# The last product split in K: ten chunks the ordinary way, six in seven block products of eight

## The chip, the cores and the metric

One core of one Trainium2 chip runs the whole program. The metric is the device time of one execution in microseconds (us). Five engines run their own instruction streams in order and wait for each other by semaphores: PE (matrix products, into accumulators in PSUM), DVE and ACT (elementwise work), POOL, and SP, whose queue issues the transfers here.

## The reference, cut to what matters

```
def reference(**kwargs):
    attn_out = _attn_ref(q, k, v)          # (2, 12, 448, 64), causal
    x = attn_out as (896, 768)             # 896 tokens, 768 features
    a = x @ w_a ; b = x @ w_b              # 768 -> 1536
    x = (a * b) @ w_out                    # 1536 -> 768
    h = x @ w_in                           # 768 -> 2048
    g = h * (1.0 / (1.0 + np.exp(-h)))
    return (g @ w_out2).astype(np.float32) # 2048 -> 768, the last product
```

The weights come as 64-bit floats and the result is 32-bit.

## The kernel before, in words

Features lie on the 128 partitions and tokens along the free dimension. The 896 tokens are two halves of 448 (`b` = 0, 1), a chunk is 128 features, so the last product has `NG` = 16 chunks of K and `NP` = 6 chunks of output. After the attention come four stages of products: 1 (`w_ab`), 2 (`w_mid`), 3 (`w_in`) and 4 (`w_out`, the last product). Every factor is held as two parts, a high and a low one, and each product of a chunk is three matmuls of 128x128 weights against 128x448 (high by high, high by low, low by high; L296).

Work on PE is cut into **granules**: two output chunks (`m`, `m+1`) and some chunks of K. There are two kinds.

- **Plain** (`plain`): for each chunk of K, two weight tiles by two token halves by three matmuls, 12 in all, into four accumulators that stay open over all granules of the same `m`. Stage 4 is all of this kind: for each of three `m`, four granules of four chunks. At the end of an `m`, `ending` copies each accumulator (L939, ACT) and sends it out (L940, SP queue). While `m` is 0, `hand_over` makes the high part (L771, ACT) and the low part (L774, DVE) of every chunk of activations, two chunks ahead of their use.
- **Fast** (`quad`): six chunks of K are three pairs, the two output chunks and the two token halves make the other two dimensions of a 2x2 block product, and seven products of blocks do the work of eight: 7 x 3 chunks x 3 matmuls = 63 instead of 72. Stage 3 and most of stage 1 are of this kind. It needs sums of activation blocks, split in high and low parts (`ACTS`, seven sets for each of three pairs), and sums of weight blocks (L279, L284, DVE). Its four results come out of copies of an accumulator (L319, ACT) and additions (L794, DVE). Activation sums for stage 1 are made by `sums_of`, driven by `Sums`.

The weights of each granule are loaded as raw 64-bit words (`load_ahead`, L141, SP queue) and converted two granules ahead of use: two ACT steps (L214, L220) and two DVE steps (L226, L231) for each of the two tiles, then high parts (L253, ACT) and low parts (L257, DVE). `Timeline` sets the order: its clock is the count of matmuls written so far, and each elementwise step is put into its engine's stream when its due count is reached (`CONV_F`, `CONV_X`, `CONV_Y` give the due points of the conversion as fractions of a granule) and when buffers are free (`A`, `W`, `R` and `banks` count them). The engines then run these streams in order.

Of the kernel before, what the change touches and what calls it, by code (L numbers as in the profile page):

```python
# [10 lines left out]
F32 = mybir.dt.float32  # L11
# [27 lines left out]
SUMS_MM = 3  # L39
# [9 lines left out]
POST = 9  # L49
HAND = 2  # L50
SLOT_MM = 7

CONV_F = dict(exp=(-0.06, 0.07), low=(0.01, 0.13), join=(0.20, 0.29), sign=(0.37, 0.45), t13=0.54, t24=0.62,
              wa=(0.58, 0.72), wd=(0.62, 0.80), wc=(0.74, 0.90), wb=(0.85, 1.0),
# [2 lines left out]
              wa=(0.44, 0.54), wd=(0.48, 0.59), wc=(0.56, 0.65), wb=(0.61, 0.71))  # L57
CONV_Y = dict(exp=(-0.54, -0.17), low=(-0.50, -0.10), join=(-0.22, 0.30), sign=(-0.14, 0.36), t13=0.62, t24=0.72,
              wa=(0.60, 0.80), wd=(0.66, 0.86), wc=(0.86, 0.98), wb=(0.93, 1.04))

@with_exitstack
def fused_kernel(ctx: ExitStack, tc: tile.TileContext, qk, v, w_ab, w_mid, w_in, w_out, out):
# [19 lines left out]
    NKB = (S + P - 1) // P  # L84
    NF, NG = w_ab.shape[0], w_in.shape[0]
    KP = NP // 2
    H = NP * P
    toks = [slice(b * S, (b + 1) * S) for b in range(B)]

# [10 lines left out]
    class Ring:  # L100


        def __init__(self, pools, sizes, shape, tag="t"):
            self.pools, self.room, self.shape, self.tag, self.home = pools, list(sizes), shape, tag, {}
# [295 lines left out]
    def sums_of(c):  # L400
# [40 lines left out]
        rest()  # L441
        A.free(s4)

    class Sums:


        def __init__(self):
            self.gens, self.need = [], 1

        def step(self):  # L450
            if not self.gens or self.need > A.left() - SPARE:
                return
            self.need = next(self.gens[0], None)
            if self.need is None:
                self.gens.pop(0)
                self.need = 1
                self.step()

        def go_on(self):
            self.step()  # L460
            if self.gens:
                line.after(SUMS_MM, self.go_on)

    sums_x = Sums()

    granules = []

    def granule(src, n, fast, **more):
        granules.append({"src": src, "n": n, "fast": fast, "length": 7 * 3 * KP if fast else 12 * n, **more})
# [7 lines left out]
    for m in range(0, NG, 2):  # L477
        granule([w_in[m], w_in[m + 1]], NP, True, stage=3, m=m)
    for m in range(0, NP, 2):
        for k in range(0, NG, 4):  # L480
            granule([w_out[m + i, :, k:k + 4] for i in range(2)], 4, False, stage=4, m=m, k=k, K=NG)

    for g in granules:
        if g["stage"] == 3 and g["m"] in (0, 2):
            g["due"] = (CONV_X, CONV_Y)[g["m"] // 2]
    loads += [(g, src) for g in granules for src in g["src"]]

    with tc.manual_schedule():  # L490
# [328 lines left out]
        def gate_put(g):  # L819
            def put(i, j, t):  # L820
                key = (g["m"] + j, i)
                psum = id(t) in banks.home
                if g["s"] == 0:
                    t_f[key] = t
                    if psum:
                        t_f[key] = copy_of(t, "ga")
                        banks.free(t)
                    return
                src = t[:, 0:S] if psum else t
                nc.vector.tensor_tensor(out=t_f[key], in0=src, in1=t_f[key], op=ALU.mult)  # L830
                (banks if psum else A).free(t)
            return put

        def silu_put(g):
            def put(i, j, t):
                key = (g["m"] + j, i)
                psum = id(t) in banks.home

                def act():
                    if psum:  # L840
                        g_f[key] = A.new(F32, "gf")
                        nc.scalar.activation(out=g_f[key], in_=t[:, 0:S], func=AF.Silu)
                        banks.free(t)
                    else:
                        nc.scalar.activation(out=t, in_=t, func=AF.Silu)
                        g_f[key] = t
                line.after(6 if i == 0 and j == 0 or psum else 3, act)
            return put

        def plain(g, accs, f, s, order, done):  # L850


            for bs, tiles in order:
                for k in range(g["n"]):
                    kk = g["k"] + k
                    if f and g["m"] == 0 and kk + HAND < g["K"]:
                        for b in range(B):
                            hand_over(f, s, (kk + HAND, b), 6 + 3 * b)
                    for i in tiles:
                        wh, wl = (t[:, k] for t in g["w"][i])  # L860
                        for n in range(3):
                            for b in bs:
                                ah, al = s[kk, b]
                                l, r = ((wh, ah), (wh, al), (wl, ah))[n]
                                mm(accs[i][b], l, r, kk == 0 and n == 0, kk == g["K"] - 1 and n == 2)
                        line.tick(3 * len(bs))
                    if g["m"] == NP - 2 and tiles[-1] == 1:
                        for b in bs:
                            A.free(*s.pop((kk, b)))
                for b in bs:  # L870
                    for i in tiles:
                        done(b, i)
            for t in g["tiles"].values():
                W.free(*t)
# [7 lines left out]
        for at, g in enumerate(granules):  # L882
            used += g["length"]
            if at + 2 < len(granules):
                line.convert(granules[at + 2], used - LEAD, granules[at + 1]["length"])
            load_ahead()
            stage, m = g["stage"], g["m"]
            if g["fast"]:
                f, s = (t_f, t_s) if stage == 1 else (g_f, g_s)
                last = at + 1 < len(granules) and not granules[at + 1]["fast"]  # L890
                if last:
                    for k in range(HAND):
                        for b in range(B):
                            line.after(42 + 6 * k + 3 * b, partial(hand_over, f, s, (k, b), 6))
                quad(g, gate_put(g) if stage == 1 else silu_put(g), last)
                continue
            if stage == 1:

                put, bs = gate_put(g), [0, 1]
                accs = [[None, None], [None, None]]  # L900
                if at == 0:
                    bs = [1]
                    for i in range(2):
                        line.after(6 * i, partial(put, 0, i, first[i]))
                for i in range(2):
                    for b in bs:
                        accs[i][b] = banks.new(F32, "acc")
                plain(g, accs, None, XS, [(bs, (0, 1))] if at == 0 else [((0, 1), (0,)), ((0, 1), (1,))],
                      lambda b, i: line.after(3 * b, partial(put, b, i, accs[i][b])))
                if at == 1:  # L910
                    line.to(line.now)
                    for k in range(0, NP, 2):
                        A.free(*XS[k, 1])
                continue
            f, s = (t_f, t_s) if stage == 2 else (g_f, g_s)
            last, end = m == NP - 2, g["k"] + g["n"] == g["K"]
            if g["k"] == 0:
                accs = [[banks.new(F32, "acc") for _ in range(B)] for _ in range(2)]
            def ending(b, i, acc, m=m, last=last):
                src = acc[:, 0:S]  # L920
                if stage == 2:
                    todo = []
                    combine(m // 2, f"A{b + 1}{i + 1}", src, keep, todo)
                    n = 0

                    def pay():
                        nonlocal n
                        if todo:
                            todo.pop(0)()
                            n += 1  # L930
                        if todo:

                            line.after(3 if not last else 12 if n > 1 and len(todo) == 1 else 0, pay)
                        else:
                            banks.free(acc)
                    pay()
                    return
                o = A.new(F32, "o")
                nc.scalar.copy(out=o, in_=src)  # L939
                nc.sync.dma_start(out=out[m + i, :, toks[b]], in_=o)  # L940
                A.free(o)
                banks.free(acc)

            def done(b, i):
                if end:
                    line.after(0 if last else (2 * b + i) * 6, partial(ending, b, i, accs[i][b]))
                    if last:
                        line.to(line.now)

            plain(g, accs, f, s, [((0,), (0, 1)), ((1,), (0,)), ((1,), (1,))] if last and end else [((0, 1), (0, 1))],  # L950
                  done)
# [43 lines left out]
```

## Time and profile before

| | |
|---|---|
| median of 3 runs | 561.45 us (561.14 to 562.01) |
| profiled execution | 561.41 us, its span 559.6 us |
| PE busy | 552.7 us, 99% of the span |
| DVE, ACT busy | 427.8 us (76%), 375.3 us (67%) |
| granted TensorE clock, mean | 0.999 |

The profiled execution's own time lies 1.81 us over the span, which runs from its first to its last recorded instruction or transfer. Durations of single matmuls overlap the next one, so the distance from start to start tells what one costs. The same holds for DVE and ACT: a step's duration is longer than the distance to the next step's start.

### The profile page before, as it was taken

The numbers are of one execution on the slowest core, as the hardware profiler recorded it, in microseconds if no ns is written. First come the engines' busy times: TensorE is split into PE (matmuls) and PEld (weight loads), VectorE is DVE, ScalarE is ACT, GpSimd is POOL, SyncE is SP. The second block draws the span as 40 slices with busy tenths as digits, with TensorE's granted clock in tenths as the row PEclk, the third lists the DMA queues.
The fourth block names the chain that finished last, engine by engine and source line by source line (L and its number), as shares of the span: only waits on it lengthen the run. The fifth ranks groups of instructions, "written<-read, shape, count | busy, mean of one in ns | idle before, by whom it ended". The sixth has DMA issues, their size and how long they took to land.

```text
span 559.6 us, 8368 instructions
## 1 busy us (share of the span) xinstructions
PE 552.7 (99%) x2978; PEld 493.6 (88%) x2978; DVE 427.8 (76%) x811; ACT 375.3 (67%) x736; POOL 72.2 (13%) x127
## 2 busy tenths in 40 slices
PE   8999999999999999999999999999999999999997
PEld 6777767999999999999999999999999999999996
DVE  5899998998989889879682888888885896442600
ACT  5989897756666666678654566877776995632601
POOL 5888874000000000000000000000000000000000
PEclk9999999999999999999999999999999999999999
DMA  7336323044333333333333342333332242631501
GB/s 248 121 113 216 116 83 126 1 132 164 123 145 115 114 112 114 112 114 112 114 112 114 112 147 80 113 114 119 143 126 83 76 152 76 216 117 45 168 0 66
DMA packets 18089, 65.41 MB, mean 117 GB/s; under 512 B 2176, under 2 KB 6784, under 8 KB 18048
## 3 DMA queue, kind: packets, MB, share of 16 engines
q1 hardware_dynamic: 18048, 64.89, 34.3%
q8 instruction: 23, 0.38, 0.3%
q14 instruction: 18, 0.15, 0.1%
HBM read 62.13 MB, written 2.75 MB: 116 GB/s over the span
## 4 chain that ended last, share of the span: by engine, by line
PE 94%; DVE 3%; issue 1%; POOL 1%; ACT 1%; DMA 1%; SPq 0%; DVEq 0%; ACTq 0%; POOLq 0%
PE acc L296 83%; PE pt L653 4%; PE xo L665 3%; PE sc L581 3%; PE sc L585 2%; DVE sm L604 1%; POOL p L621 1%; DMA k<-qk 1%; DVE ql L556 0%; DVE kl L556 0%; ACT p L608 0%; ACT ptr L746 0%; DVE wgbl L257 0%; SPq L539 0%; DVE sums L617 0%
## 5 line engine op out<-in xcount | busy, mean ns | idle before, releaser
L226 DVE SCALAR_TENSOR_TENSOR wq<-wr 128x768 uint32<-128x768 uint32 (+1 forms) x76 | 66.4, 875 | 26.2 <-ACT wr L220 25.4
L319 ACT COPY s<-acc 128x448 f32<-128x448 f32 x72 | 38.4, 533 | 60.2 <-PE acc L296 59.8
L220 ACT ACTIVATE wr<-wr,wbias 128x768 uint32<-128x768 uint32 (+1 forms) x76 | 69.8, 918 | 0.0
L214 ACT ACTIVATE wr<-wr 128x768 f32<-128x768 f32 (+1 forms) x76 | 63.8, 840 | 3.3 <-DMA wr<-w_out 1.8
L231 DVE SCALAR_TENSOR_TENSOR wq<-wr,wq 128x768 uint32<-128x768 uint32 (+1 forms) x76 | 63.8, 872 | 0.1
L621 POOL TENSOR_SCALAR p<-p,rcp 128x448 f32<-128x448 f32 (+6 forms) x84 | 56.2, 685 | 16.8 <-DVE rcp L618 7.3
L608 ACT ACTIVATE p<-sm,nmax 128x448 f32<-128x448 f32 (+6 forms) x84 | 42.0, 508 | 11.4 <-DVE nmax L604 10.8
L296 PE MATMUL acc<-th,wgbl 128*128 128x448 f32 x168 | 49.6, 366 | 0.0
L296 PE MATMUL acc<-tl,wgbh 128*128 128x448 f32 x168 | 49.4, 366 | 0.0
L296 PE MATMUL acc<-th,wgbh 128*128 128x448 f32 x168 | 49.4, 366 | 0.0
L296 PE MATMUL acc<-th,wgal 128*128 128x448 f32 x168 | 49.4, 365 | 0.0
L296 PE MATMUL acc<-tl,wgah 128*128 128x448 f32 x168 | 49.4, 365 | 0.0
L296 PE MATMUL acc<-th,wgah 128*128 128x448 f32 x168 | 49.3, 365 | 0.0
L604 DVE CUSTOM_DVE_ANT_0 sm<-sc,mask 128x448 f32<-128x448 f32 (+6 forms) x84 | 31.4, 417 | 6.0 <-PE sc L585 5.0
L296 PEld LDWEIGHTS acc<-th,wgbh 128*128 128x128 f32 x168 | 31.5, 188 | 2.9 <-DVE s L794 0.2
L296 PEld LDWEIGHTS acc<-th,wgah 128*128 128x128 f32 x168 | 31.6, 188 | 2.8
L296 PEld LDWEIGHTS acc<-th,wgbl 128*128 128x128 f32 x168 | 31.6, 188 | 2.6
L296 PEld LDWEIGHTS acc<-tl,wgah 128*128 128x128 f32 x168 | 31.5, 188 | 2.6
L296 PEld LDWEIGHTS acc<-th,wgal 128*128 128x128 f32 x168 | 31.6, 188 | 2.5
L296 PEld LDWEIGHTS acc<-tl,wgbh 128*128 128x128 f32 x168 | 31.5, 188 | 2.5
L257 DVE TENSOR_TENSOR wgal<-wq,wgah 128x512 fp32r<-128x512 f32 (+1 forms) x20 | 16.0, 802 | 23.1 <-ACT wgah L253 14.4
L653 PE MATMUL pt<-ident,p 128*128 128x128 f32 x192 | 27.8, 282 | 2.2 <-POOL p L621 1.3
(166 smaller groups left out, 1380.6 us busy)
## 6 DMA issues: line engine op xcount, KB each, us to landing
wr<-w_ab SPq DMA_DIRECT2D x24, 768.0 KB, 4.7
wr<-w_in SPq DMA_DIRECT2D x16, 768.0 KB, 4.9
wr<-w_out SPq DMA_DIRECT2D x24, 512.0 KB, 4.3
wr<-w_mid SPq DMA_DIRECT2D x12, 768.0 KB, 4.5
v<-v SPq DMA_DIRECT2D x12, 256.0 KB, 3.0
q<-qk SPq DMA_DIRECT2D x24, 112.0 KB, 2.9
k<-qk SPq DMA_DIRECT2D x12, 224.0 KB, 2.9
out<-o SPq DMA_DIRECT2D x12, 224.0 KB, 3.6
```

The source lines that it names most:

```text
L214: nc.scalar.activation(out=word(i, 1).bitcast(F32), in_=word(i, 1).bitcast(F32), func=AF.Copy, scale=2.0 ** -112)
L220: nc.scalar.activation(out=word(i, 0), in_=word(i, 0), func=AF.Relu, bias=wbias, scale=2.0 ** -29)
L226: nc.vector.scalar_tensor_tensor(out=xi(i), in0=word(i, 1), scalar=3, in1=word(i, 0), op0=ALU.logical_shift_left, op1=ALU.bitwise_or)
L231: nc.vector.scalar_tensor_tensor(out=xi(i), in0=word(i, 1), scalar=0x80000000, in1=xi(i), op0=ALU.bitwise_and, op1=ALU.bitwise_or)
L296: nc.tensor.matmul(out=acc[:, 0:S], lhsT=w, rhs=a, start=first, stop=last, skip_group_check=True)
L319: nc.scalar.copy(out=t, in_=acc[:, 0:S])
L581: nc.tensor.matmul(out=sc, lhsT=t[a][:, j - BIG].rearrange("p h q -> p (h q)"), rhs=t[k][:, 0:K], start=(i == 0), stop=(i == 2))
L604: nc.vector.tensor_tensor_reduce(out=sm, in0=sc, in1=mask[:, S - K:S], op0=ALU.add, op1=ALU.min, scale=-(D ** -0.5), scalar=3.0e38, accum_ ...
L608: nc.scalar.activation(out=p_sb[u % 2][j][:, 0:K], in_=sm, func=AF.Exp, bias=t["nmax"][:, c:c + 1], scale=-1.0, accum_out=t["sums"][:, c:c ...
L621: nc.gpsimd.tensor_scalar(out=pj, in0=pj, scalar1=t["rcp"][:, COL[j]:COL[j] + 1], scalar2=1.0, op0=ALU.mult, op1=ALU.mult,)
L653: nc.tensor.transpose(out=place[j, kb], in_=p_sb[u % 2][j][:, kb * P:(kb + 1) * P], identity=ident)
L665: nc.tensor.matmul(out=t["x"][h * D:(h + 1) * D, kb * P:S], lhsT=t["v"][:, kb, h * D:(h + 1) * D], rhs=t["pt"][:, kb, h, kb * P:S], start= ...
```

## The change

The last product is cut in K. Its first ten chunks (`N4` = `NG` - `NP` = 10) stay plain, in granules of four and six chunks for each of the three `m`; their sums are no longer sent out but copied to tiles `o` that stay on chip (`parts`). After all plain granules come three fast granules, one for each `m`, over the last six chunks. `out_put` adds each fast result to its `o` (L914, DVE) and sends it out. A new generator, `sums_last`, makes the activation sums of the six chunks while the plain granules run, driven by a second `Sums`; these six chunks need no `hand_over`. `CONV_Z` sets the due points of one conversion.

```
+PUT_MM = 20
+START_G = 60
+PACE_G = 3
+SPARE_G = 3
...
+CONV_Z = dict(exp=(0.02, 0.15), low=(0.09, 0.22), join=(0.35, 0.45), sign=(0.50, 0.58), ghi=(0.64, 0.72), glo=(0.78, 0.86))
...
+    N4 = NG - NP
...
+    def sums_last(c, f):
+
+        a11, a12, a21, a22 = (f.pop((N4 + 2 * c + i, b)) for b in range(B) for i in range(2))
...
+        yield 1
+        s3 = add(a11, a21, ALU.subtract)
+        yield 2
+        rest = halves_of(s3, 7)
+        yield 1
+        s1 = add(a21, a22, ALU.add)
+        A.free(a21)
+        yield 0
+        rest()
+        A.free(s3)
+        yield 2
+        rest = halves_of(a22, 4)
+        yield 1
+        s2 = add(s1, a11, ALU.subtract)
...
+        rest = halves_of(s1, 5)
+        yield 1
+        s4 = add(a12, s2, ALU.subtract)
...
+        for t, n in ((a11, 1), (a12, 2), (s2, 6), (s4, 3)):
+            yield 2
+            rest = halves_of(t, n)
+            yield 0
+            rest()
+            A.free(t)
...
-            if not self.gens or self.need > A.left() - SPARE:
+            if not self.gens or self.need > A.left() - self.spare:
...
-                line.after(SUMS_MM, self.go_on)
-
-    sums_x = Sums()
+                line.after(self.pace, self.go_on)
+
+    sums_x, sums_g = Sums(), Sums(SPARE_G, PACE_G)
...
     for m in range(0, NP, 2):
-        for k in range(0, NG, 4):
-            granule([w_out[m + i, :, k:k + 4] for i in range(2)], 4, False, stage=4, m=m, k=k, K=NG)
+        for k, n in ((0, N4 - 6), (N4 - 6, 6)):
+            granule([w_out[m + i, :, k:k + n] for i in range(2)], n, False, stage=4, m=m, k=k, K=N4)
+    for m in range(0, NP, 2):
+        granule([w_out[m + i, :, N4:] for i in range(2)], NP, True, stage=4, m=m)
...
+        if g["stage"] == 4 and g["m"] == 0 and not g["fast"] and g["k"]:
+            g["due"] = CONV_Z
...
+        parts = {}
+
+        def out_put(g):
+            def put(i, j, t):
+                key = (g["m"] + j, i)
+                psum = id(t) in banks.home
+
+                def add():
+                    o = parts[key]
+                    nc.vector.tensor_tensor(out=o, in0=t[:, 0:S] if psum else t, in1=o, op=ALU.add)
+                    (banks if psum else A).free(t)
+                    nc.sync.dma_start(out=out[key[0], :, toks[i]], in_=o)
+                    A.free(o)
+
+                line.after(0 if psum or g["m"] == NP - 2 else PUT_MM, add)
+                line.to(line.now)
+            return put
...
-                quad(g, gate_put(g) if stage == 1 else silu_put(g), last)
+                quad(g, (gate_put, None, silu_put, out_put)[stage - 1](g), last)
...
+            if stage == 4 and g["k"] == m == 0:
+                def begin():
+                    sums_g.gens += [sums_last(c, g_f) for c in range(KP)]
+                    sums_g.go_on()
+                line.after(START_G, begin)
...
-                o = A.new(F32, "o")
-                nc.scalar.copy(out=o, in_=src)
-                nc.sync.dma_start(out=out[m + i, :, toks[b]], in_=o)
-                A.free(o)
+                parts[m + i, b] = copy_of(acc, "o")
                 banks.free(acc)
```

Line numbers are shifted in the changed kernel: the matmul is L302, the conversion's ACT steps are L220 and L226, its DVE steps L232 and L237, `hand_over` is L826 and L829, the copy of an accumulator L325, the addition in `quad` L849; new are the additions and splits of `sums_last` (L456 on DVE, L461 on ACT, L462 on DVE) and L914. The instructions up to the first granules of stage 4 are in the same order in both kernels.

**First place: ACT at the start of stage 4.** `th` are the high parts of the first chunks, `wr` raw weights under conversion, `s` results of stage 3. Before:

```order
L319 COPY s_4668<-acc 128x448
L220 ACTIVATE wr<-wr,wbias 128x512
L771 CAST th<-s_3826 128x448
L214 ACTIVATE wr<-wr 128x512
L771 CAST th<-s_3860 128x448
L220 ACTIVATE wr<-wr,wbias 128x512
L845 ACTIVATE s_4668<-s_4668 128x448
L771 CAST th<-s_3909 128x448
L771 CAST th<-gf 128x448
```

With the change:

```order
L325 COPY s_4667<-acc 128x448
L220 ACTIVATE wr<-wr 128x768
L826 CAST th<-s_3826 128x448
L826 CAST th<-s_3860 128x448
L226 ACTIVATE wr<-wr,wbias 128x768
L220 ACTIVATE wr<-wr 128x768
L900 ACTIVATE s_4667<-s_4667 128x448
L226 ACTIVATE wr<-wr,wbias 128x768
L826 CAST th<-s_3909 128x448
L826 CAST th<-gf 128x448
```

The two last rows are the high parts of chunk 2: four conversion steps of 768 now stand between the copy and them, where three of 512 stood.

The same place on DVE with the change: `tl` are the low parts, `wq` the weights as 32-bit floats, and the rows end with both low parts of chunk 2.

```order
L829 TENSOR_TENSOR tl<-s_3860,th 128x448
L849 TENSOR_TENSOR s_4635<-acc,s_4635 128x448
L232 SCALAR_TENSOR_TENSOR wq<-wr 128x768 x2
L829 TENSOR_TENSOR tl<-s_3909,th 128x448
L237 SCALAR_TENSOR_TENSOR wq<-wr,wq 128x768
L829 TENSOR_TENSOR tl<-gf,th 128x448
```

One of the two conversion steps L237, which stood together ahead of the low parts, now stands between them.

**Second place: ACT where the fast granules of stage 4 begin.** Before there are none, and at the end of an `m` (here the first) the copies of results stand among conversion steps:

```order
L939 COPY o<-acc 128x448 x2
L253 CAST wgah<-wq 128x512
L939 COPY o<-acc 128x448
L253 CAST wgbh<-wq 128x512
L939 COPY o<-acc 128x448
```

With the change, at the end of the last plain `m`; `p1h` to `p7h` are high parts of the activation sums, `s_5419` is the first copy of the first fast granule:

```order
L461 CAST p1h<-s_4605 128x448
L325 COPY o<-acc 128x448 x2
L461 CAST p2h<-s_4635 128x448
L325 COPY s_5419<-acc 128x448
L325 COPY o<-acc 128x448
L461 CAST p6h<-S 128x448
L325 COPY o<-acc 128x448
L461 CAST p3h<-S 128x448
```

The last four parts of the third pair of chunks stand behind copies that wait for PE; on DVE `p6l<-S,p6h` needs `p6h`.

**Third place: the end.** Before, ACT ends with four copies, each followed by a transfer:

```order
L214 ACTIVATE wr<-wr 128x512
L220 ACTIVATE wr<-wr,wbias 128x512
L253 CAST wgah<-wq 128x512
L253 CAST wgbh<-wq 128x512
L939 COPY o<-acc 128x448 x4
```

With the change the results end on DVE:

```order
L849 TENSOR_TENSOR s_5699<-s_5688,s_5699 128x448
L914 TENSOR_TENSOR o<-s_5699,o 128x448
L849 TENSOR_TENSOR s_5676<-acc,s_5676 128x448
L914 TENSOR_TENSOR o<-s_5676,o 128x448
L914 TENSOR_TENSOR o<-acc,o 128x448
```

The last copy on ACT has become an addition on DVE out of the accumulator, behind four others.

## Rows read from the trace of the kernel before

**Rows 1.** Page, head and part 1: busy us, share of the span, instructions.

```profile
span 559.6 us, 8368 instructions
PE 552.7 (99%) x2978; PEld 493.6 (88%) x2978; DVE 427.8 (76%) x811; ACT 375.3 (67%) x736; POOL 72.2 (13%) x127
```

**Rows 2.** Chain that ended last, in order of time: start, us, what; its end.

```profile
98.67 457.62 PE acc L296 x2250
556.29 0.02 issue
556.31 0.53 ACT o L939
```

**Rows 3.** Timeline of PE (start, us, engine, line): first and last of stage 4.

```profile
438.97 0.57 PE L296 MATMUL acc<-th,wgah 128*128 128x448 f32 x2
...
555.91 0.37 PE L296 MATMUL acc<-th,wgbl 128*128 128x448 f32 x1
```

**Rows 4.** Timeline of ACT: the same copy in two neighbouring fast granules of stage 3.

```profile
402.63 0.53 ACT L319 COPY s<-acc 128x448 f32<-128x448 f32 x1 [0.21 <-PE acc L296]
...
415.42 0.54 ACT L319 COPY s<-acc 128x448 f32<-128x448 f32 x1 [0.22 <-PE acc L296]
```

**Rows 5.** Windows of stage 4: stretch, length, busy of each engine, PEclk, DMA share, GB/s.

```profile
440.00:500.00 60.00, 60.00 (x297) 55.31 (x296) 42.02 (x72) 40.92 (x75) 0.00 (x0) 1.00 0.41 138
500.00:540.00 40.00, 40.00 (x198) 36.95 (x197) 14.23 (x22) 14.22 (x24) 0.00 (x0) 1.00 0.28 89
540.00:559.60 19.60, 16.27 (x81) 14.68 (x79) 0.00 (x0) 2.13 (x4) 0.00 (x0) 0.98 0.13 47
```

**Rows 6.** Timeline of DVE: steps of 768, 384, 448 and 512 back to back.

```profile
406.38 0.95 DVE L257 TENSOR_TENSOR wal<-wq,wah 128x768 fp32r<-128x768 f32 x1
407.24 0.55 DVE L257 TENSOR_TENSOR wdl<-wq,wdh 128x384 fp32r<-128x384 f32 x1
407.71 0.95 DVE L257 TENSOR_TENSOR wcl<-wt,wch 128x768 fp32r<-128x768 f32 x1
...
441.34 0.62 DVE L774 TENSOR_TENSOR tl<-s,th 128x448 fp32r<-128x448 f32 x1
441.87 0.62 DVE L774 TENSOR_TENSOR tl<-gf,th 128x448 fp32r<-128x448 f32 x1
...
448.32 1.29 DVE L231 SCALAR_TENSOR_TENSOR wq<-wr,wq 128x512 uint32<-128x512 uint32 x2
449.52 0.61 DVE L774 TENSOR_TENSOR tl<-s,th 128x448 fp32r<-128x448 f32 x1
```

**Rows 7.** Timeline of ACT: conversion steps of 768, high parts, and a copy.

```profile
410.37 0.92 ACT L214 ACTIVATE wr<-wr 128x768 f32<-128x768 f32 x1
411.18 0.98 ACT L220 ACTIVATE wr<-wr,wbias 128x768 uint32<-128x768 uint32 x1
412.05 0.91 ACT L214 ACTIVATE wr<-wr 128x768 f32<-128x768 f32 x1
...
434.12 0.57 ACT L771 CAST th<-s 128x448 fp32r<-128x448 f32 x1
434.59 0.68 ACT L214 ACTIVATE wr<-wr 128x512 f32<-128x512 f32 x1
...
435.62 0.53 ACT L319 COPY s<-acc 128x448 f32<-128x448 f32 x1
436.04 0.78 ACT L220 ACTIVATE wr<-wr,wbias 128x512 uint32<-128x512 uint32 x1
```

**Rows 8.** Group of instructions by line and shape, 400 to 560: xcount | busy, mean ns.

```profile
L794 DVE TENSOR_TENSOR s<-acc,s 128x448 f32<-128x448 f32 x7 | 4.3, 618 | 2.5 <-PE acc L296 2.5
```

**Rows 9.** Timeline of ACT and the transfer queue at the end; DMA issues there.

```profile
550.82 1.14 ACT L939 COPY o<-acc 128x448 f32<-128x448 f32 x2 [15.02 <-PE acc L296]
...
551.38 5.82 SPq L940 DMA_DIRECT2D out<-o  x4
...
out<-o SPq DMA_DIRECT2D x4, 224.0 KB, 1.9
```

More of the change, by code (lines that the diff above doesn't have):

```diff
@@ L442, in sums_of, with add, halves_of, __init__ @@
         A.free(s4)
+    def sums_last(c, f):
+        a11, a12, a21, a22 = (f.pop((N4 + 2 * c + i, b)) for b in range(B) for i in range(2))
+        def add(a, b, op):
+            t = A.new(F32, "S")
+            nc.vector.tensor_tensor(out=t, in0=a, in1=b, op=op)
+            return t
+        def halves_of(t, n):
+            hi, lo = ACTS[n][c] = A.new(F32R, f"p{n}h"), A.new(F32R, f"p{n}l")
+            nc.scalar.copy(out=hi, in_=t)
+            return lambda: nc.vector.tensor_tensor(out=lo, in0=t, in1=hi[:].bitcast(F32), op=ALU.subtract)
+        yield 1
[14 more added lines that the diff above has]
+        rest()
+        A.free(a22)
+        yield 2
+        rest = halves_of(s1, 5)
+        yield 1
+        s4 = add(a12, s2, ALU.subtract)
+        yield 0
+        rest()
+        A.free(s1)
+        for t, n in ((a11, 1), (a12, 2), (s2, 6), (s4, 3)):
+            yield 2
+            rest = halves_of(t, n)
+            yield 0
+            rest()
+            A.free(t)
     class Sums:
-        def __init__(self):
-            self.gens, self.need = [], 1
+        def __init__(self, spare=SPARE, pace=SUMS_MM):
+            self.gens, self.need, self.spare, self.pace = [], 1, spare, pace
         def step(self):
-            if not self.gens or self.need > A.left() - SPARE:
+            if not self.gens or self.need > A.left() - self.spare:
                 return
@@ L889, in fused_kernel @@
                 f, s = (t_f, t_s) if stage == 1 else (g_f, g_s)
-                last = at + 1 < len(granules) and not granules[at + 1]["fast"]
-                if last:
+                last = at + 1 == len(granules) or not granules[at + 1]["fast"]
+                if last and stage < 4:
                     for k in range(HAND):
@@ L915, in fused_kernel @@
             f, s = (t_f, t_s) if stage == 2 else (g_f, g_s)
-            last, end = m == NP - 2, g["k"] + g["n"] == g["K"]
+            last, end = m == NP - 2 and stage == 2, g["k"] + g["n"] == g["K"]
+            if stage == 4 and g["k"] == m == 0:
[3 more added lines that the diff above has]
+                line.after(START_G, begin)
             if g["k"] == 0:
```

## The prediction

> **What bounds the kernel now.** Read first the busy shares on the page [rows 1], then the chain that ended last, in order of time [rows 2], then the windows of the stage that is changed [rows 5]. The shares say that PE is busy in 99% of the span. That alone could hide slow stretches, since pipelined matmuls overlap; the chain settles it. From 98.67 us to 556.29 us it is nothing but matmuls of L296, one after the other, and only a copy and a transfer follow [rows 2]. So in the last product the end is set by the count of matmuls times their distance from start to start. Stage 4 has 16 chunks x 12 matmuls x 3 values of `m` = 576 of them; the first starts at 438.97, the last at 555.91 [rows 3]. That is 575 distances in 116.94 us, 203.4 ns each, with no loss to be seen. The windows add that the other engines have room there: over 440 to 559.6 us DVE works 42.0 + 14.2 = 56.3 us and ACT 40.9 + 14.2 + 2.1 = 57.3 us [rows 5], and most of that lies ahead of 500 us. The granted clock is 1.00 in both full stretches, the higher level of 2.4 GHz [rows 5].
>
> The sum is made against the profiled execution, 561.41 us, which is 0.04 us under the median of 561.45 us; I carry no correction for that.
>
> **The change, PE.** Plain granules now hold ten chunks: 10 x 12 x 3 = 360 matmuls. Three fast granules add 3 x 63 = 189. Together 549, so 27 fewer. Is a matmul of a fast granule as cheap as a plain one? Two neighbouring fast granules of stage 3 have the same copy at 402.63 and 415.42 [rows 4]: 12.79 us for 63, 203.0 ns each. So 216 plain matmuls x 203.4 ns = 43.93 us go, 189 x 203.0 ns = 38.37 us come: **5.56 us** less on the path.
>
> The Trainium skill, page "TensorE: Matmul & The Clock Gate", section "Back-to-back issue gap", gives a warm spacing of N/2.4 + 2.5 ns, an estimate of 189 ns for 448 columns; 27 of these are 5.1 us, and the forecast would be 556.4 us by it. The measured 203 ns differs from it, and the measurement decides.
>
> **The change, the end.** Before, the last copy on ACT starts 0.40 us after the last matmul's start [rows 2, 3] and takes 0.53 us [rows 2]. Now a DVE addition out of the accumulator stands there, 0.618 us for the nearest row, an addition from an accumulator in `quad` [rows 8]: **+0.09 us**. Four DVE steps stand ahead of it (third place of the order). The two that add product 3 become possible 9 matmuls = 1.83 us before PE is done and take about 0.62 + 0.05 + 0.62 = 1.3 us; the other two belong to a product that ended 18 matmuls = 3.7 us before. So DVE waits for PE, not the reverse. The last transfer of 224 KB lands 1.9 us after its issue [rows 9], as before. The transfer ahead of it now comes some 1.2 us earlier instead of 2.4; but of the four transfers before two stood just as close, behind two copies that took 1.14 us together, and the median to landing is still 1.9 us [rows 9]. Cost nothing.
>
> **The change, DVE and ACT in total.** Distances from start to start on DVE: 0.86 us for a step of 768, 0.47 for 384, 0.53 for 448, (449.52 - 448.32)/2 = 0.60 for 512 [rows 6]. Before, stage 4 wants 32 low parts (17.0 us) and 12 conversions of six steps of 512 (43.2): 60.2 us, less the first conversion, which is done ahead of it (3.6): 56.6, against 56.3 measured. That agrees, so the same sum may be made of after: 20 low parts 10.6; three conversions with 512, 10.8; three with 768, 18 x 0.86 = 15.5; three for fast granules, each 7 x 0.86 + 5 x 0.47 = 8.4, so 25.1; activation sums, three times 4 additions and 7 low parts, 33 x 0.53 = 17.5; results, 3 x 7 additions x 0.53 = 11.1. Together 90.6, less 3.6: 87 us in a stage of 111.4 us, 78%. ACT has 12 fewer high parts but 21 for the sums and 12 more copies, and larger conversions; it ends near 70 us. No engine but PE is full over the stage, so what can cost time is the order at single places. I work out the two tightest.
>
> **Tight place one, start of stage 4** (first place of the order). PE reaches chunk 2 after 24 matmuls, at 438.97 + 4.88 = 443.85, and its fourth matmul needs the second low part at 443.85 + 0.61 = 444.46. ACT: the copy at 435.62 is set by PE and the next step starts at 436.04 [rows 7]. Then, with 0.81 us for L214 and 0.87 for L220 at 768 [rows 7] and 0.47 for a high part [rows 7], which I also take for the activation among them: 0.81 + 2 x 0.47 + 0.87 + 0.81 + 0.47 + 0.87 = 4.77, so 440.81; two high parts, the second done at about 441.85. DVE: its second L226 step (L232 after) waits for that last L220, about 440.95, then 0.86 (441.81), a low part (442.34), L231 (443.20), the second low part done by 443.82. PE wants it at 444.46: **0.6 us to spare**. Before it was done at 442.49, from the row at 441.87 [rows 6], 2 us to spare. So this cover shrinks, but holds; chunk 4, behind the rest of this conversion, is about as close. Price if I am off: a tenth more on these nine microseconds would make PE wait 0.3 us, twice 0.6.
>
> **Tight place two, first fast granule** (second place of the order). Call the end of the last plain granule P, 438.97 + 360 x 0.2034 = 512.2. ACT's copy `s_5419` waits for nine matmuls and starts at P + 1.83 + 0.2; one copy of `o` (0.42, the distance at 435.62 [rows 7]) and then `p6h` (0.57 us long) follow, done at P + 3.4 or 3.5, and the low part `p6l` on DVE by P + 4.15. PE takes `p6l` of the third pair with its 26th matmul of the granule, at P + 25 x 0.203 = P + 5.08: **0.9 us to spare**. `p2l` by the same count has 1.5. The copies of accumulators within fast granules have the nine matmuls of another product to hide behind, as in stage 3, where the distance of 203.0 ns [rows 4] leaves no room for a wait.
>
> Waits therefore: forecast 0, lower bound 0, since stage 4 before shows no loss that could come back; upper bound for small misses about 1 us, both tight places late by half a microsecond.
>
> The **forecast**: 561.41 - 5.56 + 0.09 = 555.94, say 555.9 us.
>
> **The rivals.** (a) *DVE and ACT come late in places, and part of the gain becomes waits of PE.* For: DVE goes from 56 to 87 us, and during the first 25 us of the stage and again around the first fast granule it has hardly a pause; my margins are 0.6 and 0.9 us. Against: they are positive from row to row, and DVE's total leaves 24 us. Waits of 1 to 4 us give 557 to 560 us.
>
> (b) *Slower: the sums of the third pair come late.* They need buffers that come free only while PE consumes the last plain granules, so their last four splits stand just ahead of the first fast granule. If they ran one after another behind P, not beside PE, with conversion steps between them: 4 x (0.57 + 0.62) + 4 x 0.86 = 8.2 us of wait, 555.9 + 8.2 = 564.1 us. It decides from 5.5 us of waits on. For: three of those splits do stand behind copies that wait for PE. Against: PE needs them spread over 6, 15, 24 and 51 matmuls after P, and the first is split ahead of P in the order.
>
> (c) *Within 0.2% of before: the saving isn't on the path.* If fast matmuls were dearer, 549 at 213 ns would use up all of it. The distance in stage 3 speaks against it [rows 4], and the granted clock has no reason to fall while PE works on. 561 us.
>
> **How the numbers follow.** Forecast 0.85, (a) 0.09, (b) 0.04, (c) 0.02. About 0.2%, 1.1 us, is what a measurement of this kernel can tell from no change. The forecast and (a) are faster by more than that: 0.94; same 0.02; slower 0.04. The runs of before spread from 0.3 us under to 0.6 us over their median, which gives 555.4 to 556.5 around the forecast; the lower end of the range allows a little more, 555.3; above I add the upper bound for small misses and the cheaper part of (a): 557.6.
>
> **What the profile after would show.** Chain: matmuls without a break to the end, then one DVE addition. Timeline of PE: 549 matmuls from 438.97 in 111.5 us, last one starting near 550.3. No wait of PE for DVE or ACT in the list of waits after 439 us; if there is one, it names `tl` in the first ten microseconds (place one) or `p2`, `p6` near 514 to 517 us (place two). DVE busy near 87 us from 440 to the end. It would be wrong if the distance in the fast granules were over 205 ns, if DVE's additions at the end queued, or if PE lost a microsecond or more at one of the two places.

## The result and the profile after

| | before | changed kernel |
|---|---|---|
| median | 561.72 us (4 runs, 561.14 to 562.01) | 556.05 us (4 runs, 555.77 to 556.29) |
| ratio | | 0.990, 95% interval 0.9883 to 0.9917 |
| profiled execution, its span | 561.41 us, 559.6 us | 556.24 us, 554.5 us |

The forecast was 555.9 us in a range of 555.3 to 557.6. The page's head and its first part answer to [rows 1]:

```profile
span 554.5 us, 8327 instructions
PE 547.2 (99%) x2951; PEld 488.7 (88%) x2951; DVE 458.0 (83%) x853; ACT 386.5 (70%) x745; POOL 72.1 (13%) x127
```

PE has 27 matmuls less, DVE 42 steps more, and DVE's share rises from 76% to 83%. The end of the chain in order of time answers to [rows 2]:

```profile
98.88 451.96 PE acc L302 x2223
...
550.86 0.62 DVE o L914
```

It is still one stretch of matmuls, ended by one addition on DVE. On the timeline this addition is

```profile
550.86 0.62 DVE L914 TENSOR_TENSOR o<-acc,o 128x448 f32<-128x448 f32 x1 [0.53 <-PE acc L302]
```

First and last matmul of stage 4, on the timeline of PE, answer to [rows 3]:

```profile
439.11 0.57 PE L302 MATMUL acc<-th,wgah 128*128 128x448 f32 x2
...
550.47 0.36 PE L302 MATMUL acc<-p4h,wcl 128*128 128x448 f32 x1
```

548 distances in 111.36 us are 203.2 ns each, with no gap; before it was 575 in 116.94. The windows of the stage answer to [rows 5], with the same columns (length, then PE, PEld, DVE, ACT and POOL busy, PEclk, DMA share, GB/s):

```profile
440.00:500.00 60.00, 60.00 (x297) 55.48 (x296) 47.79 (x75) 44.08 (x76) 0.00 (x0) 1.00 0.37 120
500.00:540.00 40.00, 40.00 (x198) 36.92 (x198) 34.68 (x55) 22.61 (x37) 0.00 (x0) 1.00 0.25 91
540.00:554.50 14.50, 10.83 (x54) 9.67 (x52) 4.36 (x7) 2.03 (x4) 0.00 (x0) 1.00 0.27 100
```

DVE's 34.68 us in the second stretch stand where 14.23 stood, ACT's 22.61 where 14.22 stood, and PE is full beside them all the same.

### The profile page after: what moved, and what is told of

Its sections match the earlier page's. It is cut to its first block, busy times and chain, and to the rows that moved or that the text cites. A ratio compares the mean times of both kernels' runs of the same rounds, so it can differ in the third digit from the quotient of the medians.

```text
span 554.5 us, 8327 instructions
## 1 busy us (share of the span) xinstructions
PE 547.2 (99%) x2951; PEld 488.7 (88%) x2951; DVE 458.0 (83%) x853; ACT 386.5 (70%) x745; POOL 72.1 (13%) x127
## 4 chain that ended last, share of the span: by engine, by line
PE 94%; DVE 3%; issue 1%; POOL 1%; ACT 1%; DMA 1%; SPq 0%; DVEq 0%; ACTq 0%; POOLq 0%
PE acc L302 83%; PE pt L708 4%; PE xo L720 3%; PE sc L636 3%; PE sc L640 2%; DVE sm L659 1%; POOL p L676 1%; DMA k<-qk 1%; DVE ql L611 0%; DVE kl L611 0%; ACT p L663 0%; ACT ptr L801 0%; DVE wgbl L263 0%; SPq L594 0%; DVE sums L672 0%
## 5 line engine op out<-in xcount | busy, mean ns | idle before, releaser
L325 ACT COPY s<-acc 128x448 f32<-128x448 f32 x84 | 44.8, 534 | 75.5 <-PE acc L302 75.1
L232 DVE SCALAR_TENSOR_TENSOR wq<-wr 128x768 uint32<-128x768 uint32 (+1 forms) x70 | 65.1, 934 | 19.2 <-ACT wr L226 19.0
L226 ACT ACTIVATE wr<-wr,wbias 128x768 uint32<-128x768 uint32 (+1 forms) x70 | 68.2, 974 | 0.0
L220 ACT ACTIVATE wr<-wr 128x768 f32<-128x768 f32 (+1 forms) x70 | 62.7, 896 | 2.1 <-DMA wr<-w_mid 1.4
L237 DVE SCALAR_TENSOR_TENSOR wq<-wr,wq 128x768 uint32<-128x768 uint32 (+1 forms) x70 | 63.4, 932 | 0.1
L302 PE MATMUL acc<-th,wgbl 128*128 128x448 f32 x132 | 38.6, 366 | 0.0
L302 PE MATMUL acc<-th,wgal 128*128 128x448 f32 x132 | 38.5, 366 | 0.0
L302 PE MATMUL acc<-th,wgbh 128*128 128x448 f32 x132 | 38.5, 366 | 0.0
L302 PE MATMUL acc<-tl,wgbh 128*128 128x448 f32 x132 | 38.5, 365 | 0.0
L302 PE MATMUL acc<-tl,wgah 128*128 128x448 f32 x132 | 38.5, 365 | 0.0
L302 PE MATMUL acc<-th,wgah 128*128 128x448 f32 x132 | 38.4, 365 | 0.0
L849 DVE TENSOR_TENSOR s<-acc,s 128x448 f32<-128x448 f32 x42 | 25.9, 618 | 5.2 <-PE acc L302 5.2
L708 PEld LDWEIGHTS pt<-ident,p 128*128 128x128 f32 x192 | 20.5, 141 | 10.5 <-POOL p L676 5.7
L302 PEld LDWEIGHTS acc<-th,wgbh 128*128 128x128 f32 x132 | 24.8, 188 | 2.2 <-DVE s L849 0.2
L302 PEld LDWEIGHTS acc<-th,wgah 128*128 128x128 f32 x132 | 24.8, 188 | 2.2
L302 PEld LDWEIGHTS acc<-th,wgbl 128*128 128x128 f32 x132 | 24.8, 188 | 2.0
L302 PEld LDWEIGHTS acc<-th,wgal 128*128 128x128 f32 x132 | 24.8, 188 | 2.0
L302 PEld LDWEIGHTS acc<-tl,wgah 128*128 128x128 f32 x132 | 24.8, 188 | 1.9
```

What stands on the lines that cost most here:

```text
L220: nc.scalar.activation(out=word(i, 1).bitcast(F32), in_=word(i, 1).bitcast(F32), func=AF.Copy, scale=2.0 ** -112)
L226: nc.scalar.activation(out=word(i, 0), in_=word(i, 0), func=AF.Relu, bias=wbias, scale=2.0 ** -29)
L232: nc.vector.scalar_tensor_tensor(out=xi(i), in0=word(i, 1), scalar=3, in1=word(i, 0), op0=ALU.logical_shift_left, op1=ALU.bitwise_or)
L237: nc.vector.scalar_tensor_tensor(out=xi(i), in0=word(i, 1), scalar=0x80000000, in1=xi(i), op0=ALU.bitwise_and, op1=ALU.bitwise_or)
L302: nc.tensor.matmul(out=acc[:, 0:S], lhsT=w, rhs=a, start=first, stop=last, skip_group_check=True)
L325: nc.scalar.copy(out=t, in_=acc[:, 0:S])
```

## The experiments

All seven start from the changed kernel. The comparison is with its median, 556.05 us, and with that of the kernel before on the same chip.

**1. The matmuls put back.** Is it the 27 matmuls, or the new order around them? The last six chunks become plain granules again, with all else that the change did to the order kept; the activations of these chunks are only split, not summed.

```
+FAST_M = ()
...
-        s3 = add(a11, a21, ALU.subtract)
...
-        for t, n in ((a11, 1), (a12, 2), (s2, 6), (s4, 3)):
+        for t, n in ((a11, 1), (a21, 8), (a12, 2), (a22, 4)):
...
-        granule([w_out[m + i, :, N4:] for i in range(2)], NP, True, stage=4, m=m)
+        granule([w_out[m + i, :, N4:] for i in range(2)], NP, m in FAST_M, stage=4, m=m,
+                **({} if m in FAST_M else dict(post=True, k=0, K=NP)))
...
+                if post:
+                    o = parts[m + i, b]
+                    nc.vector.tensor_tensor(out=o, in0=src, in1=o, op=ALU.add)
+                    nc.sync.dma_start(out=out[m + i, :, toks[b]], in_=o)
```

> The last six chunks are computed by plain granules again, after the ten, and added to the sums kept on chip; the splits of the six chunks are made at the same place as the sums were. All else is as in the changed kernel: 576 matmuls in place of 549. Theory (the gain is the 27 matmuls at 203 ns and nothing else): 556.05 + 5.5 = 561.5 us, 561.1 to 562.1, the same as before within 0.2%. Rival (the gain comes from the new order: results kept on chip, transfers out at the end, fewer steps in the first pass): the time stays under 559 us although the matmuls are back.

Measured: 561.55 us (560.89 to 561.78), before 561.67 on that chip, ratio 0.9995 (0.9985 to 1.0004). Its first and last matmul of stage 4:

```profile
438.58 0.57 PE L303 MATMUL acc<-th,wgah 128*128 128x448 f32 x2
...
555.18 0.37 PE L303 MATMUL acc<-p4h,wgbl 128*128 128x448 f32 x1
```

116.60 us for 575 distances, 202.8 ns each. The gain goes with the matmuls: 561.55 - 556.05 = 5.50 us for 27 of them, 204 ns each. On the timeline stage 4 is 116.60 - 111.36 = 5.24 us longer than in the changed kernel; between this figure and the 5.58 us against the kernel before lie a few tenths by which the same 576 matmuls differ from one trace to the other. Keeping results on chip, adding them on DVE and sending everything out at the end is worth nothing and costs nothing that this comparison can tell; its interval reaches from 0.8 us faster to 0.2 us slower.

**2. A little more work at the two tight places.** The prediction left 0.6 and 0.9 us to spare there. The trace after says what was really left. Place one, the parts of chunk 2 for the second token half, rows of ACT, DVE and PE:

```profile
441.30 0.59 ACT L826 CAST th<-gf 128x448 fp32r<-128x448 f32 x1
...
443.29 0.61 DVE L829 TENSOR_TENSOR tl<-gf,th 128x448 fp32r<-128x448 f32 x1
...
444.38 0.57 PE L302 MATMUL acc<-tl,wgah 128*128 128x448 f32 x2
```

The low part is done at 443.90; the second of the two matmuls, 0.20 us after 444.38, takes it: 0.68 us to spare. Place two, the first fast granule, where the end of the last plain granule, P in the prediction, is 512.25:

```profile
514.27 0.53 ACT L325 COPY s<-acc 128x448 f32<-128x448 f32 x1 [1.03 <-PE acc L302]
514.70 0.54 ACT L325 COPY o<-acc 128x448 f32<-128x448 f32 x1
515.13 0.58 ACT L461 CAST p6h<-S 128x448 fp32r<-128x448 f32 x1
...
515.74 0.62 DVE L462 TENSOR_TENSOR p6l<-S,p6h 128x448 fp32r<-128x448 f32 x1 [0.97 <-ACT p6h L461]
...
517.35 0.37 PE L302 MATMUL acc<-p6l,wch 128*128 128x448 f32 x1
```

`p6l` of the third pair is done at 516.36 and taken at 517.35: 0.99 us. The chain is the one laid out: a copy that waits for PE, a copy of a result, the high part, the low part. The edit repeats steps there, shorter than what is left:

```
+PAD_D = (224,)
+PAD_A = (448,)
...
+            for w in PAD_A * (n == 6 and c == KP - 1):
+                nc.scalar.copy(out=hi[:, 0:w], in_=t[:, 0:w])
...
+                for w in PAD_D * (f is g_f and key == (2, 0)):
+                    nc.vector.tensor_tensor(out=lo[:, 0:w], in0=t[:, 0:w], in1=hi[:, 0:w].bitcast(F32), op=ALU.subtract)
```

> Both tight places get a repeated step that is shorter than what the trace of the changed kernel leaves there: a half-wide repeat (224 columns, about 0.4 us) of a low part of chunk 2 on DVE, where 0.68 us are to spare, and one repeat of p6h of the third pair on ACT (about 0.6 us), where 0.99 us are to spare. Theory (cover hides it): 556.0 us, within 0.3 of the changed kernel, and no matmul waits. Rival (DVE and ACT set the pace there, the margins are not real): 0.4 to 1.0 us more, with waits of PE at tl of chunk 2 and at p6.

Measured: 556.08 us (555.55 to 556.31), ratio to before 0.9896 (0.9882 to 0.9911). No matmul waits. The cover hides it: the low part of chunk 2 is now done 0.26 us ahead of its use, `p6l` 0.40 us.

**3. More work than the margins hold.** The same edit with four and six full repeats:

```
+PAD_D = (448, 448, 448, 448)
+PAD_A = (448, 448, 448, 448, 448, 448)
```

> The same two places, repeats longer than the margins: four full repeats of the low part (4 x 0.67 = 2.7 us) and six of p6h (6 x 0.62 = 3.7 us). Theory: PE waits for what exceeds the margins, 2.7 - 0.7 = 2.0 us near 444 to 447 us and 3.7 - 1.0 = 2.7 us near 517 us, together 4.7: 560.8 us, 560 to 561.5. Rival (there is much more room than I counted): under 557.5 us.

Measured: 561.03 us (560.37 to 562.91), 4.98 us more than the changed kernel. The timeline of PE, the matmuls with idle time before them:

```profile
444.70 0.47 PE L304 MATMUL acc<-tl,wgah 128*128 128x448 f32 x1 [0.63 <-DVE tl L835]
446.10 0.47 PE L304 MATMUL acc<-tl,wgah 128*128 128x448 f32 x1 [0.93 <-DVE tl L833]
521.12 0.47 PE L304 MATMUL acc<-p6h,wch 128*128 128x448 f32 x1 [2.07 <-ACT p6h L465]
521.78 0.47 PE L304 MATMUL acc<-p6l,wch 128*128 128x448 f32 x1 [0.19 <-DVE p6l L466]
```

The waits stand where they were expected. The booked idle sums to 3.8 us, and stage 4 is 5.0 us longer than in the changed kernel. The difference is how a stop is booked: idle begins at the modelled end of the last matmul, 0.16 us later than the next would have started (0.366 long, 0.203 apart), and the matmul after a stop lasts 0.47 in place of 0.37. That is 0.26 us beside the booked idle for each of the four stops, some 1.05 us, and 3.8 + 1.05 = 4.9. So both margins are real in both directions: repeats that stayed 0.26 and 0.40 us below them cost nothing, and what the longer ones had above them came back as time. Three of the ten executions (561.82, 562.88 and 562.91 us) took longer than the others (at most 561.07) at a lower mean granted clock, 0.995 to 0.996 where the others have 0.999; experiment 5 returns to that.

**4. The sums started late.** Rival (b) as an edit of one number:

```
-START_G = 60
+START_G = 180
```

> START_G is 180 in place of 60: the activation sums start 120 matmuls later (24 us), all else is the same. Theory: same matmuls, but the sums of the third pair now end beside the fast granules, and the conversion of the later fast granules is pushed back with them; laid out step by step with the traced durations PE waits some 6.6 us in all, at p1 and p7 of the first fast granule and at p7 and p3 of the second and third: 562.7 us, 560 to 564, so the whole gain is gone and the kernel may be slower than before. Rival (DVE has 24 us free in this stage, so the sums find room anywhere): under 557 us.

Measured: 562.21 us (561.77 to 562.99), ratio to before 1.0012 (1.0002 to 1.0022). The list of waits of PE over stage 4 (total, times, longest):

```profile
PE acc L302 <- ACT s L325: 2.4, 2, 1.5
PE acc L302 <- DVE p1l L462: 1.3, 2, 1.1
PE acc L302 <- DVE p7l L462: 0.8, 1, 0.8
PE acc L302 <- ACT p1h L461: 0.3, 1, 0.3
```

4.8 us of booked idle and six stops of 0.26 us make 6.4 us, enough for the 6.16 us lost, which are more than the whole gain. The stops stand in the first two fast granules, and the third waits nowhere. But this run isn't the pure case. Five of the seven sums of the third pair (1, 2, 3, 5 and 6) were not yet written into the streams when the first fast granule was, so that granule read older ones and did not wait for its own.

**5. The same with its own sums.** What is left of the sums is put out ahead of the first fast granule:

```
-START_G = 60
+START_G = 180
...
+                    ACTS[n] = [None] * KP
...
+                if stage == 4 and m == 0:
+                    line.to(line.now)
+                    sums_g.spare = 0
+                    while sums_g.gens:
+                        sums_g.step()
```

> START_G is 180 in place of 60, and what is left of the activation sums when the last plain granule is written is put into the streams of ACT and DVE at once, ahead of the first fast granule, so that every fast granule has its own sums. Theory (rival b of the prediction as a mechanism, provoked): DVE starts the third pair's sums too late, the first high and low part of p1 of the third pair come behind them, and PE waits some 4.7 us at p1 of the first fast granule and nowhere else: 560.7 us, 559.5 to 562. Rival (the 24 us that DVE has free in this stage take it up): under 557 us.

Measured: 562.71 us (561.78 to 563.35), ratio to before 1.0016 (1.0006 to 1.0025): slower than before by 1.0 us, and over the 562 us that were expected at most. PE waits only where expected, and for as long. Timeline of PE:

```profile
512.82 0.36 PE L302 MATMUL acc<-p1h,wal 128*128 128x448 f32 x1
515.89 0.47 PE L302 MATMUL acc<-p1h,wah 128*128 128x448 f32 x1 [2.72 <-ACT p1h L461]
517.83 0.74 PE L302 MATMUL acc<-p1l,wah 128*128 128x448 f32 x1 [1.47 <-DVE p1l L462]
...
521.36 0.57 PE L302 MATMUL acc<-p2l,wah 128*128 128x448 f32 x1
521.73 0.57 PE L302 MATMUL acc<-p2h,wal 128*128 128x448 f32 x1
...
524.21 0.36 PE L302 MATMUL acc<-p6h,wch 128*128 128x448 f32 x1
524.41 0.37 PE L302 MATMUL acc<-p6l,wch 128*128 128x448 f32 x1
524.62 0.36 PE L302 MATMUL acc<-p6h,wcl 128*128 128x448 f32 x1
```

From start to start, less the usual distance, the two stops are 2.87 + 1.74 = 4.6 us, against 4.7 expected. But the median lost 6.66 us, and the profiled execution, the longest of the ten, 563.35 - 556.24 = 7.1. The rest goes with the clock. After the second stop matmuls start 0.37 us apart (521.36 to 521.73), 448 columns at the lower level of 1.2 GHz, and only from 524.21 us on 0.20 apart again. The windows show it in the granted clock (PEclk):

```profile
510.00:515.00 5.00, 3.18 (x16) 2.60 (x14) 3.29 (x6) 3.06 (x7) 0.00 (x0) 1.00 0.00 0
515.00:520.00 5.00, 2.64 (x7) 2.14 (x8) 5.00 (x10) 3.76 (x9) 0.00 (x0) 0.72 0.00 0
520.00:525.00 5.00, 5.00 (x17) 4.46 (x16) 4.93 (x9) 1.73 (x3) 0.00 (x0) 0.60 0.51 154
525.00:530.00 5.00, 5.00 (x26) 4.62 (x26) 4.06 (x6) 3.86 (x7) 0.00 (x0) 1.00 0.13 50
```

Of these stretches the third is the telling one: PE is busy in all of it and starts 17 matmuls, where the fourth has 26. From 517.83 to 524.21 there are 17 distances in 6.38 us, which at 203 ns would be 3.45: 2.9 us given away without a single wait. 4.6 + 2.9 = 7.5 us, a little more than the 7.1 of this execution. All ten executions of this kernel show a mean granted clock of 0.993 to 0.997. In experiment 3 the stops were 1.6 and 2.3 us of booked idle, far apart, and in the profiled execution the granted clock stayed at 1.00 in every 5 us around them; but its three longer executions, at 0.995 to 0.996, had a lower clock behind the same program, and no trace of these was kept. So stops as in experiment 3 can do without a fall and, it seems, with one. Whether it is the length of the stops or that they stand so close together was not tried.

**6. Fewer matmuls still.** How much of this gain could be had again in the same place?

```
-    def block_product(acc, w, acts, first):
+    def block_product(acc, w, acts, first, lean=False):
...
+                if lean and n == 1:
+                    continue
...
-                for _ in block_product(acc, w[n], ACTS[n], first):
+                for _ in block_product(acc, w[n], ACTS[n], first, g["stage"] == 4):
```

> Left out: of the three matmuls of each chunk in the fast granules of the last product, the one with the low part of the activations, so 126 in place of 189, and each of the three granules lasts 8.5 us on PE in place of 12.8; DVE and ACT have all their work. Theory (only the covers of ACT and DVE limit what further matmuls could be saved there): 63 x 203 ns = 12.8 us go, but ACT and DVE come late for the copies s2, s5 of each of these granules and give some 5 us back as waits at p7 and p3: 548.5 us, 547 to 551. Rival (still bound by PE alone): 543.3 us. Rival (ACT and DVE already full in the changed kernel): 554 us or more.

Measured: 551.45 us (549.25 to 551.52), ratio to before 0.982 (0.9804 to 0.9837). The profiled execution took 549.25 us. Its waits:

```profile
PE acc L302 <- ACT s L327: 4.1, 4, 1.7
```

4.1 us and four stops of 0.26 are 5.1 us of the 12.8 given back, at p7 and p3 as laid out, but of the first two fast granules alone; the third waits nowhere. Against the profiled execution of the changed kernel 7.0 us are left, so some 0.7 more went where no wait is booked, and 0.6 of these lie behind the last matmul (it starts at 542.77, the span ends at 547.35: 4.6 us where the changed kernel has 4.0). There the additions do queue on DVE, so the last starts 0.92 us after the last matmul's start:

```profile
543.15 0.63 DVE L916 TENSOR_TENSOR o<-s,o 128x448 f32<-128x448 f32 x1
543.69 0.62 DVE L916 TENSOR_TENSOR o<-acc,o 128x448 f32<-128x448 f32 x1
```

The releaser named for the waits is ACT's copy of an accumulator, but for three of the four ACT itself had waited for DVE. Its timeline ahead of the longest:

```profile
527.83 0.51 ACT L259 CAST wdh<-wq 128x384 fp32r<-128x384 f32 x1 [1.10 <-DVE wq L237]
528.25 0.53 ACT L327 COPY s<-acc 128x448 f32<-128x448 f32 x1
```

The copy stands in the stream behind a high part that waited for DVE. Only ahead of the first and shortest wait (0.32 us) is there no such row: ACT is busy without a pause there. And DVE is busy all through these stretches, while PE is not:

```profile
525.00:530.00 5.00, 3.31 (x17) 2.67 (x15) 4.93 (x9) 1.78 (x3) 0.00 (x0) 1.00 0.25 92
530.00:535.00 5.00, 3.45 (x17) 2.90 (x16) 5.00 (x8) 2.43 (x4) 0.00 (x0) 1.00 0.21 76
```

The three other executions took 551.42 to 551.52 us, with a mean granted clock of 0.992 to 0.997 where the profiled one had 1.000. The lower clock may hold their 2.2 us, as in experiment 5, but that is not shown: 0.997 and 0.992 go with the same time, and no trace of these executions was kept. The median lies over the 551 us that were expected at most, the profiled execution inside the range. So the changed kernel is bound by PE, but with a third of the matmuls of the fast granules gone, DVE's work sets the pace at these places.

**7. The end in halves.** The last result is added and sent out in two halves:

```
-                    nc.vector.tensor_tensor(out=o, in0=t[:, 0:S] if psum else t, in1=o, op=ALU.add)
...
+                    n = 2 if psum and g["m"] == NP - 2 else 1
+                    for h in range(n):
+                        c = slice(h * S // n, (h + 1) * S // n)
+                        nc.vector.tensor_tensor(out=o[:, c], in0=t[:, c], in1=o[:, c], op=ALU.add)
+                        nc.sync.dma_start(out=out[key[0], :, i * S + c.start:i * S + c.stop], in_=o[:, c])
...
-                    nc.sync.dma_start(out=out[key[0], :, toks[i]], in_=o)
```

> The last result is added and sent out in two halves of 224 columns, so the first half's transfer starts under the second half's addition. Theory: the time behind the last matmul falls by at most 0.4 us (half of the 0.7 us that the transfer takes on the wires), less a second transfer's issue: 555.9 us, 555.6 to 556.1; a difference that the trace can show and the times hardly. Rival (two transfers cost each their own fixed time one after the other): 556.4 us or more.

Measured: 556.13 us (556.05 to 556.35). The last matmul starts at 550.20 and the span ends at 554.4: 4.2 us, where the changed kernel has 4.0. DMA issues at the end, KB each and median us to landing:

```profile
out<-o SPq DMA_DIRECT2D x2, 224.0 KB, 1.9
out<-o SPq DMA_DIRECT2D x2, 112.0 KB, 1.7
```

Half the bytes land 0.2 us sooner after their issue, but this issue comes 0.23 us later behind the last matmul, after the second half's addition and the first half's issue, so the result lands 0.05 us later. The remaining 0.13 us lie behind the landing, where SP's closing waits stand (see the next section). Neither the theory (up to 0.4 us faster) nor the rival (556.4 us or more) came true: the time is the same within what the runs can tell. So the end of the changed kernel stands as it is.

## Why the prediction was right, point by point

- **PE, 5.56 us.** Measured on the timeline 116.94 - 111.36 = 5.58 us, by experiment 1 5.50 us in the medians and 5.24 us on the timelines. The distance within fast granules, taken from stage 3 as 203.0 ns, holds in stage 4 nearly: 203.3 ns (188 distances from 512.25 to 550.47), and 203.2 over all. The Trainium skill, page "TensorE: Matmul & The Clock Gate", section "Back-to-back issue gap", gives N/2.4 + 2.5 ns as the gap of an isolated matmul, an estimate of 189 ns and so of 5.1 us for the 27, and says that for a stream of weight loads and matmuls this over-counts at large N. No run here agrees with that: the measured 202.8 to 203.4 ns lie above it, and the measurement decides.
- **The end, +0.09 us.** The addition starts 0.39 us after the last matmul's start and takes 0.62, as put. From the end of that step to the end of the span it is 3.0 us, where it was 2.8 behind ACT's copy [rows 2]. These 0.2 us were not in the sum. The order of the four additions is not it, since DVE waited 0.53 us for PE ahead of the last one (its row stands in the section on the result). The last transfer is not it either: by the records of both traces it lands 1.93 us after its issue. What differs comes behind the landing. SP passes five closing waits at the end of the program, 0.06 us apart. Before, the last transfer's was the fifth, through 0.04 us after the landing; in the changed kernel it is the second, three more follow, and the last is through 0.21 us after the landing. Experiment 1, which also ends in additions on DVE, has the same 0.21 us.
- **The totals.** DVE was put at 87 us, measured 86.8 from 440 us to the end; ACT near 70, measured 68.7.
- **Tight place one.** Put at 0.6 us to spare, measured 0.68. **Tight place two**, put at 0.9, measured 0.99. Experiments 2 and 3 show that both margins are real. Chunk 4, said to be about as close as place one, has 0.80 us: its second low part is done at 448.65 and taken at 449.45.
- **Rival (a)** did not happen: no matmul of stage 4 waits. **Rival (c)** fell with the result and experiment 1, and the mean granted clock was 1.000 in all four executions. **Rival (b)** did not happen either, but its mechanism is real: provoked, it gives 562.7 us and the other sign. It was priced at up to 8.2 us of waits; the provoked case had 4.6 us, and the slower clock brought it to 6.7 in the median. That the clock would fall behind such waits was in neither its price nor that of (a).
- **The sum.** 561.41 - 5.56 + 0.09 gave 555.9; the median is 556.05 and the profiled execution 556.24. The profiled spans differ by 5.18 us: -5.58 in stage 4, +0.14 in all that lies ahead of it (stage 4 starts at 439.11 in place of 438.97), and +0.26 behind the last matmul. One slip: a spread of 0.3 us under to 0.6 us over the median gives 555.6 to 556.5 around the forecast, not 555.4; all four executions lie inside either.

## What to carry to other kernels

Where the chain is one stretch of back-to-back matmuls, a change that takes matmuls away is worth their count times their measured distance, and the work is to show for each engine behind it that the added steps come in time. That is decided at single places, not by an engine's total: DVE had 24 us free here, and a start of its sums 24 us later still turned a gain of 5.5 us into a loss of 1. Lay the order of the two or three tightest places out step by step with durations from the trace; the two margins found so were right to a tenth of a microsecond.

## What the runs showed of the hardware that was not expected

- A stop of PE costs more than the idle that the profile books: 0.26 us more for each stop (0.16 of hidden overlap, 0.10 of a longer first matmul), by which experiment 3's 3.8 us of booked idle become 4.9.
- Behind two stops of 2.9 and 1.7 us with one matmul between them the granted clock lay at its lower level for about six microseconds after PE had begun again, at a price of 2.9 us in the profiled execution of experiment 5.
- How a program ends can cost a little behind its last transfer: SP's closing waits are 0.06 us each, and how many of them are left when the last transfer lands made 0.17 us of difference between the kernel before and the changed one.
- The distance of matmuls of 448 columns is 373 ns at 1.2 GHz, just 448 cycles, but 203 ns at 2.4 GHz, 16 ns more than 448 cycles. What sets the 203 was not tried; each of these matmuls has its own weight load of 188 ns beside it.
